# A shorter fill behind each GpSimd transfer, and the last two natural tiles in the other order

## The chip, the cores and the metric

The kernel runs on one core of a Trainium2 chip. The metric is the device time of one execution in microseconds (us). A core has five engines that run their own instruction streams and wait for each other by semaphores: PE (TensorE, matmuls; PEld is its weight load), DVE (VectorE), ACT (ScalarE), POOL (GpSimd) and SP (SyncE, which here only issues DMAs). POOL issues DMAs too: its indirect transfers, whose row addresses come from an index tile.

## The reference

Four batches of 10,048 tokens of width 128 go through agent attention (49 agents) and then through a two-level mixture of experts: the token picks one of 4 groups, then one of 4 experts in it, and goes through that expert's two matrices (128 to 1024, ReLU, 1024 to 128). Cut to its core:

```python
a2k = sm(agents, k);  agent_v = a2k @ v;  x = sm(q, agents) @ agent_v     # per batch
g_idx = argmax(x @ w_group);  e_idx = argmax(x[g] @ w_expert[g])
h = np.maximum(xg[mask_e] @ w1[g, e], 0.0);  ye = h @ w2[g, e]
out[tok_idx] = (g_w * e_w)[:, None] * ye
```

## The kernel before, in words

The expert part takes nearly all of TensorE's time. A batch has 79 blocks of 128 tokens, grouped into 20 **natural tiles** (`TILES`): tiles 0 to 18 hold four blocks (512 columns), tile 19 holds three (384 columns, and of its last block only 64 rows are tokens). Batches 0 to 2 (`LB` is 3) are run whole through their most frequent expert. The last batch is instead sorted by expert: its tokens are gathered by index into 21 **taken tiles** (`TAKEN`; 20 of four blocks, the last of one block), each with its own expert's weights.

A tile of four blocks is 8 units. `first(x, k)` makes one unit's hidden values: two matmuls into `ph`, a ReLU copy `hh` on ACT and the low half `hl` on DVE. `second(...)` makes 12 matmuls (9 for tile 19) from `hh` and `hl` into the tile's output `po`. `run` puts a unit's `second` eight units (`LAG`) behind its `first`, so a tile's output is complete only at the end of the tile that follows it. After the last tile eight `second`s are left over, and PE does them with no `first` between.

For a taken tile, `fetch` (L1200) issues one indirect transfer per block on POOL into `er`; `turn` (L1228) transposes the fetched rows on PE (`at<-ident,er`) and copies them on ACT to `ets`, which `first` reads. `run` turns the next taken tile when the current taken tile is half way. `scatter` (L1238) multiplies `po` on DVE into `oo`, issues one indirect transfer per block on POOL (L1243) to the output, and then fetches the tile that is five (`DEPTH`) further on. So POOL's queue in this stage is: 20 fetches ahead, then four scatters, four fetches, four scatters, and so on. Behind each of these 162 transfers stands a fill of a tile that nobody reads:

```python
def apart(ins):
    tc.keep_in_program_order(ins)
    tc.keep_in_program_order(pool.memset(gap, 0.0))
```

The last 7 natural tiles (`BESIDE`, tiles 13 to 19) of batch 2 are kept back and run between the taken tiles: tile 13 ahead of the first, tiles 14 to 17 after the 5th, 9th, 13th and 17th taken tile, the sixth of the list after the 21st, and the seventh last of all. Their rows go out through SP (`rows_out`, L993; tile 19 needs a second DMA, L995, for its 64 rows). After the loop each engine loads the flag `any` (L877) and branches over the general path (L1309), which these inputs don't need, and the program ends (L1429).

Of the kernel before, what the change touches and what calls it, by code (L numbers as in the profile page):

```python
# [11 lines left out]
F16 = mybir.dt.float16  # L12
# [9 lines left out]
P = 128  # L22
# [15 lines left out]
NW = len(TILES)  # L38
# [21 lines left out]
LB = B - 1  # L60
# [6 lines left out]
BESIDE = 7  # L67
# [90 lines left out]
def build(ctx, tc, qT, kT, v, agT, wr, w1, w2, cpk, out):  # L158
# [7 lines left out]
    const = ctx.enter_context(tc.tile_pool(name="const", bufs=1))  # L166
# [808 lines left out]
    def natural(b, w):  # L975

        t, n = TILES[w]
        return dict(b=b, w=w, t=t, n=n, per=1, units=FB, et=state[b]["et", w], apart=b > 0 and (b < LB - 1 or w < NW - BESIDE - 2),
                    wb=wbuf[b % 2].bitcast(F16), done=rows_out)
# [202 lines left out]

    done = [0]
    ring = []
    gap = const.tile([P, 320], F16, name="gap")

    def place(b, col):
        for lo, hi, gidx, sidx in state[b]["idx"]:
# [3 lines left out]
    def prepare(b, j, to=None):  # L1192
        wfs = state[b].get("wfs")
        state[b]["wf"] = wfs.pop(0) if wfs else weights_from(expert(state[b], "used", j, [ET.SP], NE - 1))
        ws = rt.tile([P, 2 * F], I32, name="wsg", tag="S") if to is None else to
        yield from weights_of(b, ws, to is not None and vec)
        sync.dma_start(out=wall[j], in_=ws)
        yield
# [25 lines left out]
    def weigh(x):  # L1224
        s = expert(state[x["b"]], x["name"], x["j"], [ET.SP], NE - 1)
        sync.dma_start(out=x["wi"], in_=wall[bass.ds(s, 1)].rearrange("o p f -> p (o f)"))
# [129 lines left out]
    def run(x, at=None, then=None, also=None):  # L1356

        for k in range(x["units"]):
            if then and k == FB // 2:
                turn(then)  # L1360
            pending.append(first(x, k))
            if len(pending) > LAG:
                second(*pending.pop(0))
            if also:
                next(also, None)
            if at is None:
                continue
            now = at + (k + 1) / (NW * FB)
            clock[0] = now
            for y in lanes:  # L1370
                if now > y["start"]:
                    if y["kind"] == "q":
                        advance(next(z for z in lanes if z["kind"] == "f"), 1e9)
                    prior = [z for z in lanes if z["b"] == y["b"] and (z["kind"] == "a" and y["kind"] == "q" or z["kind"] == "q" and y["kind"] == "o")]
                    part = min(1.0, (now - y["start"]) / (y["end"] - y["start"]))
                    if prior and prior[0]["gen"] and (part > 0.6 or y["b"] == LB):
                        advance(prior[0], 1e9)
                    advance(y, part if part < 1 else 1e9, False)
# [12 lines left out]
    ring.extend([wbuf[2], rt.tile([P, 2 * F], I32, name="wsg", tag="S"), wbuf[1]])  # L1391
    late.extend(fetch(LB, j, "kept") for j in range(DEPTH))
    weigh(late[0])
    beside = [natural(LB - 1, w) for w in range(NW - BESIDE, NW)]
    run(beside.pop(0), None, late[0], prepare(LB, 1, wbuf[1]))
    for j in range(TAKEN):
        x = late.pop(0)
# [35 lines left out]
```

## Time and profile before

| | us |
|---|---|
| median of 3 runs | 928.49 (925.86 to 932.83) |
| the profiled execution | 927.01 |
| its span, first to last instruction | 925.2 |
| PE busy | 884.6 (96%) |
| DVE busy | 686.1 (74%) |
| ACT busy | 601.1 (65%) |
| POOL busy | 507.8 (55%) |

The busy times are sums over the whole span. The kernel has stages with different loads: POOL is busy 2 to 7 tenths of most of the span, and 8 tenths in the last quarter, where the taken tiles run. The mean granted TensorE clock was 0.994 of full speed.

### The profile page before, as it was taken

The page shows a single profiled execution, that of the slowest core. Times are in us where ns is not written, and L with a number is a line of the kernel's source. Part 1 is how long each engine was busy: PE and PEld are TensorE (multiplying, and loading weights), DVE is VectorE, ACT ScalarE, POOL GpSimd, SP SyncE. Part 2 cuts the span into 40 slices and gives each one's busy share as a digit, 9 for nine tenths or more (in the row PEclk, how much of TensorE's full clock was granted, in tenths as well). Part 3 has the DMA queues.
Part 4 walks back from the last instruction along what each step waited for, and adds up shares of the span by engine and source line. Part 5 has one row for each costly group of instructions (what it writes and reads, how often), then busy time and mean ns, then how long its engine had stood idle before and what let it go on. Part 6 is the DMA issues. An engine that isn't in the chain of part 4 may idle for free.

```text
span 925.2 us, 30602 instructions
## 1 busy us (share of the span) xinstructions
PE 884.6 (96%) x12815; PEld 703.9 (76%) x12815; DVE 686.1 (74%) x1340; ACT 601.1 (65%) x1094; POOL 507.8 (55%) x799
## 2 busy tenths in 40 slices
PE   7889999999999999999999999999999999998996
PEld 6667877787868878787777788767777777776785
DVE  7799889866798765689674667999766666664663
ACT  5486686787668768867773987565555555554552
POOL 2242475364027447415731863135778888888883
PEclk9999999999999999999999999999999999999998
DMA  9682355640168462017853301262353343433331
GB/s 343 226 287 92 91 162 157 195 149 17 39 225 292 128 200 79 25 39 251 295 172 97 112 21 39 110 218 70 118 185 128 126 145 113 133 121 118 119 100 40
DMA packets 61925, 129.03 MB, mean 139 GB/s; under 512 B 7063, under 2 KB 38889, under 8 KB 58321
## 3 DMA queue, kind: packets, MB, share of 16 engines
q1 hardware_dynamic: 56592, 119.75, 38.7%
q0 software_dynamic: 5184, 7.23, 2.9%
q8 instruction: 102, 1.67, 0.8%
q14 instruction: 47, 0.38, 0.1%
HBM read 93.83 MB, written 33.29 MB: 137 GB/s over the span
## 4 chain that ended last, share of the span: by engine, by line
PE 58%; DVE 18%; POOL 4%; ACT 3%; DMA 2%; issue 2%; SPq 0%; POOLq 0%; DVEq 0%; ACTq 0%
PE po L142 29%; PE ph L142 19%; PE at L142 11%; DVE hl L142 8%; POOL out L1243 1%; DVE oh L142 1%; ACT hh L142 1%; POOL gap L1222 1%; DMA er<-erow,gidx 1%; POOL er L1206 1%; DMA xf<-kT 1%; DVE rx L142 1%; DVE oa L142 1%; DMA w2f<-w 1%; DVE oo L142 0%
## 5 line engine op out<-in xcount | busy, mean ns | idle before, releaser
L142 DVE SCALAR_TENSOR_TENSOR hl<-ph,hh 128x512 f16<-128x512 f32 (+1 forms) x642 | 430.2, 679 | 175.7 <-ACT hh L142 174.9
L142 PEld LDWEIGHTS <-hh 128*128 128x128 f16 x5088 | 415.1, 97 | 146.7 <-issue 1.3
L142 ACT ACTIVATE hh<-ph 128x512 f16<-128x512 f32 (+1 forms) x642 | 373.3, 595 | 184.6 <-PE ph L142 180.7
L142 PE MATMUL po<-wbuf,hh 128*128 128x128 f16 x4640 | 451.6, 219 | 1.1 <-DVE wbuf L142 1.1
L142 PE MATMUL po<-wbuf,hl 128*128 128x128 f16 x2320 | 417.8, 219 | 0.0
L142 PE MATMUL ph<-et,wbuf 98*128 98x512 f16 (+1 forms) x960 | 282.1, 376 | 7.5 <-DVE hl L142 5.9
L261 POOL TENSOR_TENSOR xl<-xf,xh 128x256 f16<-128x256 f32 x280 | 178.5, 671 | 177.6 <-ACT xh L142 175.8
L142 PEld LDWEIGHTS <-hl 128*128 128x128 f16 x2544 | 247.7, 97 | 2.2 <-issue 1.3
L142 ACT ACTIVATE xh<-xf 128x1024 f16<-128x1024 f32 x78 | 81.7, 1047 | 42.8 <-PE at L142 24.4
L142 PEld LDWEIGHTS <-wbuf 98*128 98x128 f16 x1184 | 90.0, 99 | 20.6 <-issue 17.9
L988 POOL TENSOR_TENSOR oo<-oo,cw 128x256 f32<-128x256 f32 (+1 forms) x62 | 42.0, 699 | 101.6 <-ACT oo L142 91.8
L1206 POOL DMA_INDIRECT er<-erow,gidx x81 | 83.2, 1027 | 19.1 <-issue 13.8
L1243 POOL DMA_INDIRECT out<-oo,sidx x81 | 80.8, 998 | 19.1 <-issue 11.7
L142 PE MATMUL ph<-ets,wbuf 98*128 98x512 f16 (+1 forms) x224 | 64.2, 372 | 0.0
L646 POOL TENSOR_TENSOR rows<-ef,rows 128x147 f16<-128x147 f32 (+1 forms) x108 | 42.6, 424 | 39.4 <-ACT rows L142 39.4
L1222 POOL MEMSET gap<- 128x320 f16 x162 | 62.5, 386 | 0.1
L142 PEld LDWEIGHTS <-xh 128*128 128x128 f16 x1264 | 56.1, 97 | 4.9 <-issue 3.4
L142 PEld LDWEIGHTS <-xl 128*128 128x128 f16 x632 | 50.4, 96 | 3.0 <-POOL xl L261 1.9
L142 PE MATMUL at<-agh,xl 128*128 128x49 f16 x545 | 51.0, 185 | 1.4 <-POOL xl L261 1.4
L142 PE MATMUL at<-agh,xh 128*128 128x49 f16 x545 | 51.4, 185 | 1.0 <-DVE hl L142 1.0
L142 PE MATMUL at<-agl,xh 128*128 128x49 f16 x545 | 51.0, 185 | 0.0
L142 PE MATMUL at<-vf,S 128*49 128x129 f32 (+1 forms) x632 | 43.9, 278 | 2.6 <-ACT S L142 2.5
(291 smaller groups left out, 895.2 us busy)
## 6 DMA issues: line engine op xcount, KB each, us to landing
xf<-qT SPq DMA_DIRECT2D x38, 512.0 KB, 3.7
vf<-v SPq DMA_DIRECT2D x36, 516.0 KB, 5.0
xf<-kT SPq DMA_DIRECT2D x35, 512.0 KB, 7.0
out<-oo SPq DMA_DIRECT2D x57, 256.0 KB, 3.7
wbuf<-wall SPq DMA_DIRECT2D x14, 1024.0 KB, 4.8
wsg<-wall SPq DMA_DIRECT2D x7, 1024.0 KB, 5.4
erow<-rows SPq DMA_DIRECT2D x3, 1975.0 KB, 8.9
w2f<-w SPq DMA_DIRECT2D x6, 512.0 KB, 4.8
```

Of the source, the lines that this page charges most:

```text
L142: y = f(*a, **k)
L261: eng.tensor_sub(out=xl[:, y], in0=xf[:, y], in1=xh[:, y])
L646: (vec if whole else pool).tensor_sub(out=rows[:, w, NA:2 * NA], in0=ef[:, y], in1=rows[:, w, 0:NA])
L988: pool.tensor_mul(out=o[:, y], in0=o[:, y], in1=state[b]["cw"][:, t + y.start:t + y.stop].broadcast_to([P, y.stop - y.start, C]))
L1206: ins = pool.indirect_dma_start(out=er[:, q], out_offset=None, in_=erow[b][:, :], in_offset=bass.IndirectOffsetOnAxis(ap=place(b, col + q) ...
L1222: tc.keep_in_program_order(pool.memset(gap, 0.0))
L1243: ins = pool.indirect_dma_start(out=out, out_offset=bass.IndirectOffsetOnAxis(ap=place(x["b"], x["col"] + q)[1], axis=0), in_=o[:, q], in_ ...
```

## The change

The fill's tile has 160 columns in place of 320, and in the list of kept-back natural tiles the last two change places: tile 19 (384 columns) is run after the 21st taken tile, and tile 18 (512 columns) last of all.

```diff
-    gap = const.tile([P, 320], F16, name="gap")
+    gap = const.tile([P, 160], F16, name="gap")
...
-    beside = [natural(LB - 1, w) for w in range(NW - BESIDE, NW)]
+    beside = [natural(LB - 1, w) for w in [*range(NW - BESIDE, NW - 2), NW - 1, NW - 2]]
```

On POOL every transfer keeps its place; only the fill's size differs. At the end of DVE's stream (`hl` is a unit's low half, `oo<-po,er` the product of a taken tile, `oo<-po,cw` that of a natural tile) the pieces are these:

```order
 L142 SCALAR_TENSOR_TENSOR hl<-ph,hh 128x512 x8
 L142 TENSOR_TENSOR oo<-po,er 128x512
-L142 SCALAR_TENSOR_TENSOR hl<-ph,hh 128x512 x8
+L142 SCALAR_TENSOR_TENSOR hl<-ph,hh 128x512 x2
+L142 SCALAR_TENSOR_TENSOR hl<-ph,hh 128x384 x6
 L142 TENSOR_TENSOR oo<-po,er 128x512
-L142 SCALAR_TENSOR_TENSOR hl<-ph,hh 128x512 x2
+L142 SCALAR_TENSOR_TENSOR hl<-ph,hh 128x384 x2
 L142 TENSOR_TENSOR oo<-po,er 128x128
-L142 SCALAR_TENSOR_TENSOR hl<-ph,hh 128x384 x8
-L142 TENSOR_TENSOR oo<-po,cw 128x512
+L142 SCALAR_TENSOR_TENSOR hl<-ph,hh 128x512 x8
```

The 384-column units moved ahead of the 512-column units; the last product, behind these rows, is of 512 columns and was of 384. At the end of SP's queue (the last weight load, then the output DMAs and the branch) the piece is this:

```order
 L1226 DMA wbuf_105<-wall 128x2048
-L993 DMA out<-oo 128x4x128
 L993 DMA out<-oo 128x2x128
 L995 DMA out<-oo 64x128
+L993 DMA out<-oo 128x4x128
 L877 TENSOR_LOAD any
 L1309 COMPARE_AND_BRANCH
```

The pair of DMAs of tile 19 moved ahead of the single DMA of tile 18, which is now the last before SP's load of the flag and its branch.

## Rows read from the trace of the kernel before

**Rows 1.** Busy time by stretches: engine busy us (instructions), then clock, DMA share, GB/s.

```profile
740.00:760.00 20.00, 20.00 (x259) 15.80 (x258) 13.34 (x20) 11.54 (x20) 17.84 (x27) 1.00 0.42 139
840.00:860.00 20.00, 17.43 (x191) 13.04 (x192) 9.34 (x15) 8.85 (x15) 17.83 (x27) 0.91 0.30 91
842.00:846.00 4.00, 4.00 (x31) 2.70 (x30) 0.91 (x2) 1.79 (x3) 3.50 (x6) 0.63 0.15 49
850.00:852.00 2.00, 2.00 (x28) 1.52 (x26) 1.38 (x2) 0.98 (x3) 1.76 (x3) 1.00 0.98 411
```

**Rows 2.** Timeline of PE, the turns: start, us, operation, [idle before <-releaser].

```profile
710.31 0.39 PE L142 MATMUL at<-ident,er 128*98 128x128 f16 x4
...
728.22 0.39 PE L142 MATMUL at<-ident,er 128*98 128x128 f16 x4
...
782.40 0.39 PE L142 MATMUL at<-ident,er 128*98 128x128 f16 x4
...
791.47 0.33 PE L142 MATMUL at<-ident,er 128*98 128x128 f16 x3
...
820.44 0.39 PE L142 MATMUL at<-ident,er 128*98 128x128 f16 x4
...
838.58 0.22 PE L142 MATMUL at<-ident,er 128*98 128x128 f16 x1
840.84 0.42 PE L142 MATMUL at<-ident,er 128*98 128x128 f16 x2 [2.04 <-DMA er<-erow,gidx]
...
871.87 0.39 PE L142 MATMUL at<-ident,er 128*98 128x128 f16 x4
```

**Rows 3.** Timeline of POOL: five transfers of the taken stage.

```profile
689.48 1.03 POOL L1243 DMA_INDIRECT out<-oo,sidx  x1 [4.88 <-DVE oo L142]
...
695.64 1.05 POOL L1206 DMA_INDIRECT er<-erow,gidx  x1 [0.16 <-issue]
...
764.24 1.03 POOL L1243 DMA_INDIRECT out<-oo,sidx  x1 [0.17 <-DVE hl L142]
...
776.71 1.03 POOL L1243 DMA_INDIRECT out<-oo,sidx  x1 [0.17 <-DVE hl L142]
...
836.02 1.04 POOL L1206 DMA_INDIRECT er<-erow,gidx  x1 [1.81 <-issue]
```

**Rows 4.** POOL by lines: xcount, then busy us, mean ns, and idle before.

```profile
L1222 POOL MEMSET gap<- 128x320 f16 x162 | 62.5, 386 | 0.1
...
L1015 POOL MEMSET keep<- 128x1280 f16 x1 | 1.2, 1170 | 3.5 <-DVE oh L142 3.5
...
L1426 POOL MEMSET const-bfloat16-1.0<- 128x1 bf16 x1 | 0.1, 102 | 0.0
```

**Rows 5.** The two transfer lines: ns min/median/max, and landing of the fetches.

```profile
L1206 POOL DMA_INDIRECT er<-erow,gidx x81: 1002/1006/1485, 653.0 to 884.3; - x81
DMA to landing us min/median/max: 2.3/2.7/6.0
L1243 POOL DMA_INDIRECT out<-oo,sidx x81: 977/983/1031, 689.5 to 911.2; - x81
```

**Rows 6.** The end: DVE, SP's queue (SPq), landing of the L993 outputs.

```profile
914.08 0.68 DVE L142 TENSOR_TENSOR oo<-po,cw 128x512 f32<-128x512 f32 x1
...
917.78 0.56 DVE L142 TENSOR_TENSOR oo<-po,cw 128x384 f32<-128x384 f32 x1 [3.01 <-PE po L142]
918.36 0.40 SPq L993 DMA_DIRECT2D out<-oo  x1
918.80 1.10 SPq L995 DMA_DIRECT2D out<-oo  x1
...
L877 SPq TENSOR_LOAD <-any x1: 280/280/280, 920.0 to 920.0; - x1
L1309 SPq EVENT_SEMAPHORE  x9: 17/17/17, 922.9 to 923.5; - x9
DMA to landing us min/median/max: 2.3/2.9/8.1
```

## The prediction, written before the changed kernel was run

> **What bounds the kernel now.** I read the shares first, then the stage in which the fill stands, then that stage's waits and its end. PE is busy 96% of the span, so a change pays only where PE stands still, or after PE's last matmul. The fill runs in one stage only, from the first fetch at 653 us to about 912 us. The table by stretches shows that PE is full there at first (20.00 of 20 us at 740 to 760) and has holes later (17.43 of 20 us at 840 to 860) while POOL is equally busy in both, 17.8 of 20 us [rows 1]. So POOL was saturated all along, and PE reached the point where it had to wait for it. The timeline of the turns says for what: the turn that begins at 838.58 does one block, then idles 2.04 us for the fetched rows `er` [rows 2].
>
> The loss can be read off the starts of the turns. Two turns with one taken tile between them are 9.07 us apart when nothing stalls (782.40 to 791.47); with a natural tile in between as well, 17.91 us (710.31 to 728.22) [rows 2]. From 791.47 to 820.44 the program has one interval of each kind, 26.98 us, and took 28.97: 1.99 us lost. From 820.44 to 838.58 it has two of the first kind and took 18.14, nothing lost. From 838.58 to 871.87 it has again one of each kind and took 33.29: 6.31 us lost. Together **8.30 us**. That includes what the clock cost: after the idle stretch around 840 the granted clock was 0.63 in 842 to 846, part of it at the lower of the two levels [rows 1].
>
> POOL's own pace: four scatters and four fetches took 12.47 us (764.24 to 776.71) [rows 3], 1.559 us for each transfer: about 1.0 us of transfer, 0.386 of fill, 0.17 idle before the next [rows 3 to 5]. PE's need in the same units is (4 x 9.07 + 8.84)/4 = 11.28 us per taken tile where a natural tile stands after every fourth (8.84 = 17.91 - 9.07). POOL is slower by 1.2 us per tile, and the lead of five fetched tiles is used up after some ten.
>
> **The change part by part.** *The fill.* From the 1280-column fill (1170 ns) and the 320-column one (386 ns) a column costs 784/960 = 0.817 ns [rows 4]. 160 columns fewer are 0.131 us less: a fill of 0.255 us, a cycle of 1.428 us, 11.43 us per tile. The bounds are the one-column fill, 102 ns [rows 4], which gives at most 0.284 us of saving, and no saving at all, if POOL's next transfer could not start sooner for another reason. I take the line through the two nearest sizes.
>
> Now whether that is enough. The decisive fetch is the one for the turn after 838.58: without any stall it would come at 838.58 - 1.99 + 9.07 = 845.66. In POOL's queue this is the twelfth fetch group after the one at 695.64. Before: 695.64 + 12 x 12.47, then three more cycles (4.68) to the fourth transfer's start, 2.7 us of landing [rows 5], and one pause of 1.64 us beyond the usual 0.17 ahead of the transfer at 836.02 [rows 3]: 854.3, which is 8.6 us late. Measured were 8.30 us lost, so this account holds. After: the first scatter still waits for DVE at 689.48 (POOL was idle 4.88 us before it [rows 3], so shortening the 20 fetches ahead is worth nothing); the first later fetch starts four cycles behind, at 695.2; 695.2 + 12 x 11.43 + 4.28 + 2.7 + 1.64 = 841.0, that is 4.7 us ahead of the turn, with the pause still counted. The break-even is a cycle of (845.66 - 695.2 - 2.7 - 1.64)/(12 x 8 + 3) = 1.476 us: a saving of 0.083 us per transfer does everything, more does nothing more. So the term is **-8.3 us**, all of the loss. What is late next is nothing on this stage's path: PE then runs at 1.105 us per unit from the first turn to the end, as at 740 to 760. All 162 fills save 162 x 0.131 = 21 us of POOL, of which 8.3 count. Behind the shortened fill nothing else is queued than the next transfer.
>
> *The swap.* PE's sum of matmuls is unchanged: the same tiles, the drain is now eight times 12 matmuls in place of 9, and the `second`s that went between `first`s are the fewer. At the end three things move. DVE's last product has 512 columns, 0.68 us in place of 0.56: +0.12 [rows 6]. SP then issues one DMA (0.40) where it issued two (918.36 to 919.90, 1.54): -1.14 [rows 6]. The last transfer is the large one. SP's chain is what ends last: its flag load is at 920.0, right behind its second issue, and the semaphore steps behind its branch are from 922.9 on, while nothing waits in between but the branch [rows 6]. By that chain the swap is worth **-1.0 us**. If the landing of the output decided instead: before, the first of the two DMAs would land 2.3 us after 918.36, at 920.7; after, the large one at some 918.48 + 2.9 = 921.4 (median; 8.1 was the longest, beside heavy traffic) [rows 6]. Then the swap would cost +0.7. I take -1.0, since 921.4 is still ahead of the 921.9 at which SP's semaphore steps would come.
>
> The Trainium skill's page "Perfetto Trace Analysis", section "DMA Instruction — HWDGE (DVE, Sync)", warns that a DMA's semaphore comes only after the write is confirmed, surprisingly late where the target is HBM, and that the profiled duration does not contain it; it speaks against putting the larger output last. By that rule the sum would be 8.3 - 0.7 = 7.6 us of gain instead of 9.3. This trace shows SP not waiting for a landing there, so I keep the rows' value.
>
> **Sum.** -8.3 - 1.0 = -9.3 us on the profiled execution's 927.0: 917.7. The median of the three runs is 1.5 above that execution. If their spread comes from how the stalls fall, it goes with the stalls; if not, it stays. I put the forecast in between, at **918.3**.
>
> **The rivals.** *A. The spacing is fixed elsewhere (0.11).* If a transfer can't start sooner than 1.56 us after the last, the shorter fill turns into idle time. For it: 0.17 us of "issue" stands before nearly every transfer, so something besides the fill has a price. Against: that idle stays 0.16 to 0.17 whatever came before, and does not shrink where a transfer was longer (1.05 as against 0.98), as it would if starts were on a fixed beat [rows 3, 5]. Then only the swap counts: 926 to 927.5.
>
> *B. The transfers get longer when they come closer (0.10 for a part, 0.07 for more than the whole).* A transfer lands 2.7 us after its issue, so two are under way at a time already; a transfer issued before an earlier one is drained might stretch. If the stretch is 0.1 us of the 0.131, the cycle is 1.528 and the decisive fetch comes at 851.2, which is 5.5 us late: about 3 us of gain left from the fill, 922 to 924. **The slower side**: the stretch passes 0.131 us at the same loss as before, and at about 0.24 us (transfers of 1.24 us instead of 1.0) the loss is 99 x 0.11 = 11 us more than before, 1% slower: 937. One fetch did take 1.485 us [rows 5]; if all did, the cycle is 1.9 us and the time near 961. Against it: the medians, 1.006 and 0.983 us, lie at the minima, 1.002 and 0.977 [rows 5], and in 850 to 852, where the DMA engines were busy 98% of the time, POOL was busy 1.76 of 2 us, its usual share [rows 1].
>
> By the skill's same page, section "DMA Instruction — SWDGE (GPSIMD)", the DMA engines start on the descriptors before all are written when these are more than the buffer holds; a buffer that is not yet drained is how the stretch of B could come about. No row here shows a full buffer, and the chance stays as the rows give it.
>
> *C. The change does what it says, but the lead is eaten elsewhere.* If the landings late in the stage are nearer the longest (6.0) than the median, the decisive fetch still comes 1.4 us ahead. It is inside the main case.
>
> **How the numbers follow.** Main case 0.72: 916 to 920.5. B in part 0.10: 922 to 924. A 0.11: 926 to 927.5. B beyond the whole 0.07: above 928. The range goes from 915.5, for a median that falls with the profile and a little more, to 925, which takes in the main case and B in part: about 0.82. One per cent, about what a measurement of this kernel can tell from no change, is 9.3 us, so the line is at 919.2, inside the main case: 0.50 of its 0.72 lies below. Faster by over 1%: 0.50; within 1%: 0.22 + 0.10 + 0.11 = 0.43; slower: 0.07.
>
> **What would show it.** In the changed kernel's profile: fills of 0.25 us, still 0.17 us of idle behind them, transfers still near 1.0 us, and eight transfers in at most 11.5 us, with POOL idle now and then for DVE's `oo`. No turn waits for `er`; turns 9.07 and 17.91 us apart throughout; the clock at 1.00 in every stretch of the stage up to the last matmul. SP's load of the flag about 1.2 us after PE's last matmul instead of 2.3. If the turns still wait while the fills are at 0.25, it is A or B, and the transfers' durations and the idle before them say which. The prediction is wrong most simply if the time barely moves although the stalls are gone: then PE lost elsewhere what it gained here.

## The result, and the profile after

The changed kernel took **918.13 us** (median of 9 runs, 917.37 to 921.96), the kernel before 927.15 (9 runs, 925.86 to 932.83). The recorded ratio is 0.9898, with a 95% interval of 0.9882 to 0.9913 (the quotient of the two medians is 0.9903). The forecast was 918.3 in a range of 915.5 to 925. The profiled execution of the changed kernel took 917.81, its span is 916.0: 9.2 us under the 925.2 of before, where the prediction's sum had -9.3.

The table by stretches of the changed kernel (columns as in [rows 1]) shows the taken stage without holes:

```profile
740.00:760.00 20.00, 20.00 (x258) 15.80 (x257) 13.39 (x20) 11.49 (x20) 17.67 (x29) 1.00 0.40 136
840.00:860.00 20.00, 20.00 (x258) 15.70 (x256) 13.41 (x21) 11.11 (x20) 17.67 (x29) 1.00 0.42 137
842.00:846.00 4.00, 4.00 (x57) 3.28 (x55) 2.85 (x6) 2.31 (x4) 3.51 (x6) 1.00 0.82 286
700.00:900.00 200.00, 200.00 (x2574) 158.47 (x2571) 133.76 (x202) 113.94 (x197) 166.41 (x266) 1.00 0.38 125
```

PE is busy 20.00 of 20 us where it had 17.43, and the clock is 1.00 where it was 0.91 and, in 842 to 846, 0.63 [rows 1]. The last line is the whole stretch from 700 to 900: PE has no idle time in it. The turns of the changed kernel (columns as in [rows 2]):

```profile
710.35 0.39 PE L142 MATMUL at<-ident,er 128*98 128x128 f16 x4
...
791.52 0.39 PE L142 MATMUL at<-ident,er 128*98 128x128 f16 x4
...
818.50 0.39 PE L142 MATMUL at<-ident,er 128*98 128x128 f16 x4
...
836.64 0.39 PE L142 MATMUL at<-ident,er 128*98 128x128 f16 x4
845.71 0.39 PE L142 MATMUL at<-ident,er 128*98 128x128 f16 x4
...
881.76 0.22 PE L142 MATMUL at<-ident,er 128*98 128x128 f16 x1
```

No turn has idle time for `er` any more. From 791.52 to 818.50 are 26.98 us, the sum of the two undisturbed intervals, where [rows 2] has 28.97. The turn that was expected at 845.66 is at 845.71. From 710.35, the sixth turn, to the last one are 171.41 us; before it was 179.70 (710.31 to 890.01), so **8.29 us** of waiting are gone. The trace of the kernel before tells what they were made of (PE alone: us, PE busy, clock, DMA share, GB/s):

```profile
710.31:890.01 179.70, 174.69 (x2192) 0.99 0.38 123
842.00:844.00 2.00, 2.00 (x15) 0.50 0.18 61
```

PE stood idle for 5.0 of the 8.3 us. During the other 3.3 it counts as busy but got less done: from 842 to 844, behind the idle of 2.04 us, the granted clock was 0.50, the lower of the two levels (1.2 of 2.4 GHz), where the changed kernel has 1.00. How much of the 3.3 us is the clock's is not worked out here. "Waiting" below means the whole. On GpSimd (timeline, then two rows of its lines with mean ns in the middle):

```profile
689.52 1.03 POOL L1243 DMA_INDIRECT out<-oo,sidx  x1 [7.59 <-DVE oo L142]
...
695.15 1.05 POOL L1206 DMA_INDIRECT er<-erow,gidx  x1 [0.16 <-issue]
...
757.87 1.03 POOL L1243 DMA_INDIRECT out<-oo,sidx  x1 [0.17 <-DVE hl L142]
...
769.27 1.03 POOL L1243 DMA_INDIRECT out<-oo,sidx  x1 [0.17 <-issue]
...
823.77 1.03 POOL L1206 DMA_INDIRECT er<-erow,gidx  x1 [1.94 <-issue]
```

```profile
L1222 POOL MEMSET gap<- 128x160 f16 x162 | 40.9, 252 | 0.1
L1243 POOL DMA_INDIRECT out<-oo,sidx x81 | 80.8, 998 | 30.8 <-DVE oo L142 17.9 <-issue 12.4 <-DVE hl L142 0.5
```

The fill takes 0.252 us (0.386 before), the transfers their old 1.0, the idle behind the fill its old 0.17. Eight transfers take 11.40 us (757.87 to 769.27) in place of 12.47. The first scatter starts where it did, at 689.52, and GpSimd only waited longer for it (7.59 us): the shorter fills in the 20 fetches ahead bought nothing. The pause of nearly 2 us in the fetches is still there (1.94), and is harmless now. Last, the end of the changed kernel (DVE, then SP's queue), which answers to [rows 6]:

```profile
909.54 0.69 DVE L142 TENSOR_TENSOR oo<-po,cw 128x512 f32<-128x512 f32 x1 [4.08 <-PE po L142]
910.26 0.41 SPq L993 DMA_DIRECT2D out<-oo  x1
```

```profile
L877 SPq TENSOR_LOAD <-any x1: 286/286/286, 910.7 to 910.7; - x1
L1309 SPq EVENT_SEMAPHORE  x9: 17/17/17, 913.7 to 914.3; - x9
L1309 SPq COMPARE_BRANCH  x1: 45/45/45, 911.1 to 911.1; - x1
L1309 ACTq COMPARE_BRANCH  x1: 50/50/50, 904.2 to 904.2; - x1
L1309 ACTq EVENT_SEMAPHORE  x2: 17/17/17, 907.0 to 907.1; - x2
```

From the start of the last product to the end of the span are now 6.46 us (909.54 to 916.0); before they were 7.42 (917.78 to 925.2): **0.96 us** less. The two parts, 8.29 and 0.96, make 9.25 us; the sixth turn came 0.04 us later, and the spans differ by 9.2. On SP 2.6 us pass between the branch and the first semaphore step behind it (911.1 to 913.7). On ACT, which issues no DMA in this program, they are 2.8 (904.2 to 907.0), so SP's pause needs no landing as its reason.

### The profile page after: what moved, and what is told of

It reads as the page before. It is cut to its first block, busy times and chain, and to the rows that moved or that the text cites. A ratio compares the mean times of both kernels' runs of the same rounds, so it can differ in the third digit from the quotient of the medians.

```text
span 916.0 us, 30601 instructions
## 1 busy us (share of the span) xinstructions
PE 880.7 (96%) x12815; PEld 701.9 (77%) x12815; DVE 687.3 (75%) x1340; ACT 601.2 (66%) x1094; POOL 486.8 (53%) x799
## 4 chain that ended last, share of the span: by engine, by line
PE 62%; DVE 17%; ACT 2%; DMA 2%; issue 1%; POOL 1%; SPq 0%; ACTq 0%; POOLq 0%; DVEq 0%
PE po L142 31%; PE ph L142 20%; PE at L142 11%; DVE hl L142 8%; DMA xf<-kT 1%; DMA w2f<-w 1%; DVE oh L142 1%; DVE oa L142 1%; ACT hh L142 1%; DVE rx L142 1%; DVE wbuf L142 1%; DVE cnt L142 0%; DVE pt L142 0%; POOL rows L646 0%; DVE rd L142 0%
## 5 line engine op out<-in xcount | busy, mean ns | idle before, releaser
L142 PE MATMUL po<-wsg,hh 128*128 128x128 f16 x448 | 43.6, 219 | 0.0
```

Source lines behind the costliest of these rows:

```text
L142: y = f(*a, **k)
```

## The experiments

The theory is that of the prediction: GpSimd's cycle (transfer, fill, idle) sets how late the fetched rows come; PE waits by what the cycle exceeds a break-even of 1.476 us, about 99 times over, once for each transfer up to the decisive fetch; the end follows SP's chain of issues. The rival is that something else did it: the tile's size and what lies behind it, the landings, the clock, or the swap. Each experiment is read by the same quantities:

| kernel | fill us | cycle us | sixth to last turn | waiting | last product to end | median us | ratio to before (95%) |
|---|---|---|---|---|---|---|---|
| before | 0.386 | 1.559 | 179.70 | 8.29 | 7.42 | 927.15 | |
| changed | 0.252 | 1.425 | 171.41 | 0 | 6.46 | 918.13 | 0.9882 to 0.9913 |
| fill only | 0.252 | 1.425 | 171.38 | 0 | 7.30 | 919.58 | 0.9889 to 0.9919 |
| swap only | 0.385 | 1.556 | 179.66 | 8.25 | 6.58 | 927.62 | 0.9977 to 1.0015 |
| 16 columns | 0.133 | 1.318 | 171.46 | 0.05 | 6.52 | 918.98 | 0.9879 to 0.9931 |
| no fill | none | 1.315 | 171.41 | 0 | 6.51 | 919.45 | 0.9889 to 0.9922 |
| 224 columns | 0.305 | 1.478 | 172.39 | 0.98 | 6.61 | 920.69 | 0.9885 to 0.9929 |
| 256 columns | 0.332 | 1.507 | 174.48 | 3.07 | 6.56 | 923.69 | 0.9921 to 0.9963 |
| 480 columns | 0.518 | 1.693 | 194.85 | 23.4 | 7.48 | 942.69 | 1.0122 to 1.0170 |

Cycle is an eighth of the time between two first scatters around 760 us, waiting is what the turns took beyond 171.41. The 0.05 us of 16 columns are no wait: no turn of that profile waits for `er`, and PE is busy from the sixth turn to the last. Each ratio is to runs of the kernel before made beside that kernel; their medians were 928.1 to 928.8 us beside the experiments and 927.15 beside the changed kernel. The medians of the changed kernel, of 16 columns and of no fill differ by up to 1.3 us although these columns agree. The sixth turn was at 710.0 to 714.2 us in the profiles of the table, a scatter of the stages ahead: the first fetch, which stands before every fill, already started at 652.8 to 656.9. A difference of 1 us between two kernels is therefore read from the turns and the end of one profile each, not from the medians.

**The fill alone.** The tile keeps its 320 columns, half of them are filled; tiles in the old order.

```diff
-        tc.keep_in_program_order(pool.memset(gap, 0.0))
+        tc.keep_in_program_order(pool.memset(gap[:, 0:160], 0.0))
```

> The tile stays 320 columns wide and in its place, only its first 160 columns are filled; the order of the natural tiles is as before. Theory (GpSimd's cycle sets the stage): fills of 0.25 us, eight transfers in 11.4 us, no turn waits for the fetched rows, 8.3 us less than before, about 918.9, and an end as before (7.5 us from the last matmul to the end of the span). Rival (what counts is the smaller tile, which moves what is allocated behind it, or the swap): no change, about 927.

All of the stage's gain is there (no waiting), and none of the end's (7.30 us). The gain needs neither a smaller tile nor the swap. The end of this kernel:

```profile
909.70 0.56 DVE L142 TENSOR_TENSOR oo<-po,cw 128x384 f32<-128x384 f32 x1 [3.02 <-PE po L142]
```

```profile
910.73 1.04 SPq L995 DMA_DIRECT2D out<-oo  x1
```

```profile
L877 SPq TENSOR_LOAD <-any x1: 283/283/283, 911.8 to 911.8; - x1
```

**The swap alone.**

```diff
-    gap = const.tile([P, 160], F16, name="gap")
+    gap = const.tile([P, 320], F16, name="gap")
```

> The fill stays at 320 columns, the last two natural tiles change places. Theory: the turns wait as before (about 8 us lost), and only the end is shorter: 6.5 us from the last matmul to the end of the span in place of 7.5, so 1.0 us less than before. Rival (the landing of the last output decides the end): 0.7 us more than before.

The turns wait as before, 8.25 us. Two rows of its timeline, the turn that waits longest and the last product, then SP's load of the flag:

```profile
842.09 0.42 PE L142 MATMUL at<-ident,er 128*98 128x128 f16 x2 [2.06 <-DMA er<-erow,gidx]
```

```profile
919.02 0.69 DVE L142 TENSOR_TENSOR oo<-po,cw 128x512 f32<-128x512 f32 x1 [4.08 <-PE po L142]
```

```profile
L877 SPq TENSOR_LOAD <-any x1: 286/286/286, 920.2 to 920.2; - x1
```

The end is 0.84 us shorter. In the medians that can't be seen: the ratio's interval, 0.9977 to 1.0015, holds both 1 and the 0.9990 that 0.96 us would make. The swap's worth rests on the traces' ends.

**The last output in two DMAs.** This asks what the end follows: the issues or the landing.

```diff
-        ins = [sync.dma_start(out=..., in_=o[:, 0:nf])]
+        ins = [sync.dma_start(out=..., in_=o[:, u:z]) for u, z in ([(0, 2), (2, 4)] if b == LB - 1 and x["w"] == NW - 2 else [(0, nf)])]
```

> As the changed kernel, but the last output goes out as two DMAs of 128 KB instead of one of 256 KB. Theory (the end follows SyncE's chain of issues): one more issue, 0.44 us later flag load, span end 0.44 us later relative to the last matmul, 6.9 us in place of 6.5. Rival (the landing decides): no change or an earlier end.

From the last product to the end it is 7.06 us in place of 6.46. SP's two issues take 1.08 us where the one took 0.41, and its load of the flag comes 1.9 us after the product's start instead of 1.2:

```profile
912.16 1.08 SPq L993 DMA_DIRECT2D out<-oo  x2
```

```profile
L877 SPq TENSOR_LOAD <-any x1: 281/281/281, 913.3 to 913.3; - x1
```

The bytes are the same and the end moved by 0.60 us, about what the second issue costs (0.67 with the gap ahead of it, where 0.44 had been assumed). The rival as it was put, no later end, is out. This run alone does not rule out a landing that counts from the second, later issue. The distances speak against it: from SP's load of the flag to the end of the span are 5.2 us before, 5.3 in the changed kernel, 5.2 with the fill only, 5.4 with the swap only and 5.2 here, whether the last output has 32 KB (the 64 rows of tile 19), 256 KB or 128 KB. A landing that takes equally long at every size could not be told from SP's chain in this way; against that stands only ACT's pause of 2.8 us behind its branch, without a DMA.

**256 columns, and 224.**

```diff
-    gap = const.tile([P, 160], F16, name="gap")
+    gap = const.tile([P, 256], F16, name="gap")
```

> As the changed kernel, with a fill of 256 columns. Theory with its break-even: fill of 0.334 us, cycle 1.507 us, 99 x (1.507 - 1.476) = 3.1 us of the loss come back, so 5.2 + 1.0 us less than before, about 921. Rival (every us of GpSimd's time counts in proportion): 8.3 x 64/160 = 3.3 us from the fill, 4.3 in all, about 923. Rival (all or nothing): the 918 of the changed kernel, or the 926 of the swap alone.

> As the changed kernel, with a fill of 224 columns, near the break-even. Theory: fill of 0.308 us, cycle 1.480 us, 99 x (1.480 - 1.476) = 0.4 us of waiting at one or two turns: the changed kernel's time plus 0 to 1 us. Rival (gain in proportion to the fill): 40% of 8.3 us given back, 3.3 us above the changed kernel.

With 256 columns 3.1 us of waiting were expected and 3.07 measured; with 224 it was 0.4 and 0.98, small, but more than the account gives (0.2 at the measured cycle of 1.478). Three turns are late with 256 columns: the one at 804.44 loses 0.68 us, then the two to which the first two rows below belong lose 1.28 and 1.06. With 224 only one is late (last row). The last late turn of each is the one that the account names as decisive:

```profile
842.23 0.60 PE L142 MATMUL at<-ident,er 128*98 128x128 f16 x2 [0.78 <-DMA er<-erow,gidx]
...
852.32 0.65 PE L142 MATMUL at<-ident,er 128*98 128x128 f16 x3 [0.58 <-DMA er<-erow,gidx]
```

```profile
848.98 0.45 PE L142 MATMUL at<-ident,er 128*98 128x128 f16 x2 [0.59 <-DMA er<-erow,gidx]
```

A gain in proportion to the fill would have left 5.0 and 3.3 us of waiting. The medians alone would not have told: 923.69 lies nearer to that rival's 923 than to the account's 921, and 920.69 is 2.6 us above the changed kernel, where the rival has 3.3. In both profiles the stage simply began later (sixth turn at 714.17 and 712.72, against 710.35).

**16 columns, and none.** What is the fill for, and does the saving go on?

```diff
-        tc.keep_in_program_order(pool.memset(gap, 0.0))
```

> As the changed kernel, with no fill at all between the transfers. Theory: the saving is already complete at 160 columns, so the time is that of the changed kernel, 917 to 918.5, and GpSimd only idles longer for the products; transfers of 1.0 us and a cycle near 1.2 us if nothing else needs the spacing. Rival (transfers that come closer get longer, or idle takes the fill's place): transfers above 1.2 us or idle of 0.3 us and more before them; the time stays at 918 while the cycle is under 1.47 us, and rises above that by 99 us for each us of cycle.

> As the changed kernel, with a fill of 16 columns. Theory: fill of 0.115 us or somewhat more, cycle near 1.29 us, the time of the changed kernel, 917 to 918.5. Rival (the spacing has a floor between 1.2 and 1.4 us, or the transfers stretch): the idle of 0.17 us behind the fill or the 1.0 us of a transfer grows by what the fill loses; the time is the same either way as long as the cycle is under 1.47 us, so the rows decide.

Neither waits, and neither is faster than the changed kernel: PE has no idle time left to give back. Both medians, 919.45 without a fill and 918.98 with 16 columns, lie above the 917 to 918.5 that was expected, by no more than the scatter said above. The rows show something else. Without a fill the idle before a transfer is 0.30 us instead of 0.17 (first fence), and with 16 columns the fill and the idle behind it make 0.31 (second fence):

```profile
721.70 1.02 POOL L1243 DMA_INDIRECT out<-oo,sidx  x1 [0.30 <-issue]
723.04 1.01 POOL L1243 DMA_INDIRECT out<-oo,sidx  x1 [0.31 <-issue]
...
732.22 1.02 POOL L1243 DMA_INDIRECT out<-oo,sidx  x1 [0.30 <-DVE hl L142]
```

```profile
720.78 1.03 POOL L1243 DMA_INDIRECT out<-oo,sidx  x1 [0.18 <-issue]
721.81 0.13 POOL L1222 MEMSET gap<- 128x16 f16 x1
722.11 1.01 POOL L1243 DMA_INDIRECT out<-oo,sidx  x1 [0.18 <-issue]
```

So the cycle here does not fall below about 1.31 us, and the first 0.13 us of a fill are free. The transfers themselves do not get longer (1.0 us throughout). Rival A of the prediction has a floor in it that exists, at 1.31 us and not at 1.56.

**More fill.** The first attempt put a second fill of 40 columns behind each of 320.

```diff
-        tc.keep_in_program_order(pool.memset(gap, 0.0))
+        tc.keep_in_program_order(pool.memset(gap, 0.0)); tc.keep_in_program_order(pool.memset(gap[:, 0:40], 0.0))
```

> As the kernel before, with a second fill of 40 columns behind each fill of 320 (order of tiles as before). Theory: GpSimd's cycle grows by a fill of about 0.135 us (0.102 for the smallest plus 40 x 0.00082), so the loss grows by 99 x 0.135 = 13.4 us: about 940.5. Rival (the stalls are set by something else, the landings or the clock): under 3 us more than before.

It took 960.82 us, 20 more than expected. The edit did something else than it should: the fills did not stay with their transfers. Once in a round of eight transfers nine of them stand in a row, four of 320 columns and five of 40 (the merged row names only the 40; the second fence has them by shape, 743.3 to 746.2), with 0.71 us of idle after them. Behind each of the other seven transfers is one fill, of 320 or of 40:

```profile
743.40 2.59 POOL L1222 MEMSET gap<- 128x40 f16 x9
746.70 1.03 POOL L1243 DMA_INDIRECT out<-oo,sidx  x1 [0.71 <-DVE hl L142]
```

```profile
L1222 POOL MEMSET gap<- 128x320 f16 x4 | 1.5, 364 | 0.2
L1222 POOL MEMSET gap<- 128x40 f16 x5 | 0.7, 134 | 0.2
```

The cycle was 1.81 us and not 1.69; 36.6 us were waited, and from the last product to the end were 12.6 us, since GpSimd's last transfer started at 944.7, 0.7 us ahead of the last product. As a test of the size it is void, though with the cycle as it was the account comes near: 99 x (1.81 - 1.476) is 33 us, and 35.5 of the 36.6 were lost up to the 19th of the 21 turns (898.33); the last turn added 1.1. The clean form fills 480 columns of one byte:

```diff
-    gap = const.tile([P, 320], F16, name="gap")
+    gap = const.tile([P, 480], mybir.dt.uint8, name="gap")
...
-        tc.keep_in_program_order(pool.memset(gap, 0.0))
+        tc.keep_in_program_order(pool.memset(gap, 0))
```

> As the kernel before, with a fill of 480 columns (of one byte each, since two-byte columns find no room). Theory, with what the run with two fills taught: fill of 0.517 us if a one-byte column costs what a two-byte one does, cycle 1.690 us; the decisive turn moves to the last one, due at 881.7 without stalls, and its fetch starts at 689.48 + 124 x 1.690 + 1.64 = 900.7 and lands 2.7 later: 21.7 us late, 13.4 more than before. GpSimd's last transfer then starts near 929, close to PE's end, and its own way through the branch adds up to 2 us at the end: 940 to 943. Rival (the stalls feed on themselves through the clock, which is why two fills cost 33 us): 950 and more.

Fill 0.518 us, cycle 1.693, 942.69 us. The waiting is 23.4 us where 21.7 were expected. That the decisive turn moves to the last one, as the expectation has it, does not come out of its own formula: at a cycle of 1.690 us the fetch for the 18th turn is 22.2 us late (689.48 + 103 x 1.690 + 1.64 + 2.7 = 867.9 against 845.66), the last one 21.7. The last overtakes only above 1.72 us (36.05 us of PE's work for 21 transfers). So it was: 22.1 us were lost up to the 19th turn (885.83), and 1.3 more at the last, whose rows came into use 4.3 us after their fetch began (901.00) where 2.7 had been allowed. The end is as before (7.48 us), so the 2 us allowed for GpSimd's way out were not needed. First scatters of two rounds, then the 19th turn and the last:

```profile
770.85 1.03 POOL L1243 DMA_INDIRECT out<-oo,sidx  x1 [0.17 <-issue]
...
784.39 1.03 POOL L1243 DMA_INDIRECT out<-oo,sidx  x1 [0.17 <-issue]
```

```profile
885.83 0.39 PE L142 MATMUL at<-ident,er 128*98 128x128 f16 x4
...
905.30 0.26 PE L142 MATMUL at<-ident,er 128*98 128x128 f16 x1 [0.61 <-DMA er<-erow,gidx]
```

The rival with a clock that feeds the stalls (950 and more) is out. No version was found that beats the changed kernel: with 16 columns and without a fill the turns are the same to 0.05 us.

## Why the prediction was right

*The loss of 8.30 us, read from the starts of the turns:* 8.29 us came back: 5.0 us of idle PE and 3.3 us of slower work, the clock's dip among them.

*The price of the fill by the line through two sizes:* 0.255 us forecast, 0.252 measured; the same line gave 0.308, 0.334 and 0.517 for three other sizes, measured 0.305, 0.332 and 0.518.

*The account of the decisive fetch and its break-even at 1.476 us:* confirmed from both sides, by no waiting at 1.425 us, 0.98 us at 1.478, 3.07 at 1.507 and 8.29 at 1.559. By the slope of 99 the kernels that wait give the break-even back as 1.475 (before), 1.473 (swap only), 1.476 (256 columns) and 1.468 (224), so it is good to about 0.01 us. The count of 99 is four short: the first later fetch, held fixed at 695.2, itself starts four cycles behind the first scatter, which makes it 103 and the break-even 1.474. The rows can't tell the two apart. This, and not the 21 us that GpSimd saves, is why the gain is 8.3.

*The swap, -1.0 us by SP's chain:* 0.96 between the two profiles, 0.84 in the swap alone; the landing of the larger output (+0.7) did not decide, and splitting it moved the end by the issue's price. Over all profiles of the table the end is 7.40 us on average in the old order (three) and 6.54 in the new one (six), 0.86 less. The 1.14 us for SP hold because tile 19's second issue is dear where it comes last, 1.04 to 1.20 us in four profiles; in the seven in which tile 18 follows it took 0.51 to 0.91, and the second issue of the split output 0.62. Why that is so is not shown.

The warning of the Trainium skill's page "Perfetto Trace Analysis", section "DMA Instruction — HWDGE (DVE, Sync)", did not come into play here: with the larger output last the span ended earlier, by 0.96 us. What the rule would cost in a program that ends with a landing, no run here shows.

*The median.* The forecast put it between the profile's 917.7 and that plus 1.5; 918.13 lies there. That it came within 0.2 us is luck: with nine runs the median before is only 0.14 us above its profiled execution, 927.15 against 927.01, and the 1.5 was the scatter of three runs.

*The rivals:* A's floor lies at 1.31 us and so out of reach; B's stretch was not seen: with no fill and a cycle of 1.315 us the transfers still take 1.0 us; C did not arise, since no turn of the changed kernel waits. What stays open is what the fill is for: no run here shows a cost of leaving it out.

## What to carry to other kernels

When one engine feeds another through a queue with a lead, compare the two paces, find the transfer at which the lead is used up, and work out the break-even pace: a saving on the feeder pays only up to it, here about 0.083 of the 0.134 us saved. The loss itself is read best from the distances of a repeated event, against an undisturbed distance of the same program. At a program's end count the issues of the queue that finishes last before counting bytes.

## What the runs showed of the hardware that was not expected

Two indirect transfers of GpSimd in a row kept 0.30 us between them even with nothing in between, and a fill of up to about 0.13 us fits into that: cycle 1.315 us without a fill, 1.318 with one of 0.133. A fill's price went by columns, not bytes: 480 one-byte columns took 0.518 us, on the line of the two-byte sizes. A second DMA issue right behind the first on SP has no fixed price: 0.62 us for the second half of the split output, and for tile 19's second DMA 0.51 us without a fill, 0.91 in the changed kernel and 1.10 before [rows 6], against 0.40 for the issue ahead of it. Between the branch at the end of the program and the first semaphore step behind it 2.6 us pass on SP and 2.8 on ACT in the changed kernel.
